# A strided local attention next to a long convolution on one core: four of the ten value-projection pairs move into the first weighting group

## The chip, the cores and the metric

One core of a Trainium2 chip runs the whole kernel. The metric is the device time in microseconds (us) of one execution; the figure that counts is the median over several executions. A hardware profile of one further execution is at hand: for every instruction its engine, start and duration, and what ended the idle time before it. Engines are named as the profile names them: PE multiplies matrices (PEld is its weight load), DVE works element by element, ACT copies out of PE's accumulator banks and computes exponentials, POOL and SP mostly issue DMA transfers.

## The reference

Two independent results stand side by side in the output. Part A is an attention with 32 heads of 20 channels over 2048 positions, in which each position looks at 8 positions, 0, 2, ... 14 back. Part B is a state-space convolution, which the kernel computes through a Fourier transform.

```python
# part A: x [1, 2048, 640], wqkv [640, 1920], wo [640, 640]
H = 32; Dh = 20; W, dil = 8, 2
q, k, v = split(x @ wqkv)                                # each [1, H, S, Dh]
idx = pos[:, None] - (arange(W) * dil)[None, :]          # mask = idx >= 0
logits = einsum("bhsd,bhswd->bhsw", q, k[idx]) * Dh**-0.5   # -1e9 where masked
attn = softmax(logits)
a = einsum("bhsw,bhswd->bhsd", attn, v[idx]).reshape(B, S, D) @ wo
# part B: y = irfft(rfft(u) * rfft(K)) + u * Dskip, with K from A, B, C, log_dt
out = concatenate([a, y], axis=-1)
```

## The kernel before

Until about 340 us of the span the kernel builds the convolution's tables and spectra and projects keys and queries. The change touches only what comes after. There, two kinds of work share the engines.

**Attention.** Positions are held in two halves of 256 columns for each of four stretches of 512 positions, and the offset w (0 to 7) picks the position that is looked at. `products(1, w)` on DVE multiplies queries of the second half by shifted keys, `logits(1, w)` on PE sums them over each head into scores, which ACT copies into `lsb` after every second w. `proj_v(d)` computes two of the 20 value channels, a *pair*, with 40 matmuls on PE into a two-bank accumulator tile, and ACT copies it to the tile `v2`. `v_halo` copies the 14 columns that a stretch needs from its neighbour, again by PE and ACT.

The softmax of a half is in two pieces. `softmax_a` takes the maximum over the 8 offsets and subtracts it (four DVE instructions), and ends with the exponential on ACT. `softmax_b` sums, takes the reciprocal and multiplies (five DVE instructions) and gives the weights `at`.

The *weighting* is six groups of eight `av_step`s, one per offset. A step is one DVE multiplication of values by weights into a ring of six buffers, then 16 small matmuls on PE that add the result into two two-bank tiles `ps_o`. After the eighth step ACT copies both tiles to `o`. The groups take the columns and channel blocks (0, 256, 0, 2), (0, 128, 2, 3), (128, 128, 2, 3), (256, 128, 0, 4), (256, 256, 4, 1), (384, 128, 0, 4): first column, columns, first block of four channels, blocks. Groups one to three use the weights of the first half, the others those of the second. `out_proj(q)` gives eight pieces, each five matmuls on PE, one copy and, every second piece, a store.

**Convolution.** `Inverse.parts()` is a list of 24 *parts*: each is 12 or 8 small matmuls on PE from a loaded tile `Z` and one copy to `ysb`; every third part stores. `load(qr)` brings in a quarter of the spectrum for six parts: 15 transfers of 128 KB, on the SP queue, or split over the SP and POOL queues for the first and the last quarter.

**What sets the order.** A planner orders the instructions of each engine when the program is built, mostly by their order in the source, but it may let an instruction pass others that it expects to wait. `keep_in_program_order` takes that freedom away for one instruction; `in_order()` switches it on for all matmuls that follow. At run time every engine, and each DMA queue, works through its list in order, and a wait holds what stands behind it.

**Accumulator banks.** Two-bank tiles (`big`, for `ps_v` and `ps_o`) come from three slots in turn, single banks (`one`, for the scores, `ps_ib`, `ps_op` and the halo) from two. A slot is free again when ACT has copied it. While a weighting group holds two of the three slots, one is left for value pairs.

**Other buffers.** `wo`, the output projection's weights, takes the place of `wv`, the value weights; the last quarter of `Z` takes the place of `xT`, the transposed input. Both places become free with the last value pair.

Of the kernel before, what the change touches and what calls it, by code (L numbers as in the profile page):

```python
# [10 lines left out]
A = mybir.AluOpType  # L11
ACT = mybir.ActivationFunctionType
AX = mybir.AxisListType
bf16 = mybir.dt.bfloat16
f32 = mybir.dt.float32

NCH = 5
# [385 lines left out]
class Attention:  # L403
# [146 lines left out]
    def softmax_b(self, hf):  # L550
        nc, lsb = self.nc, self.lsb[hf]
        TT = lambda o, a, b, op: nc.vector.tensor_tensor(out=o, in0=a, in1=b, op=op)
        tr = self.ta.tile([128, 4, 256], f32, name="tree", tag="TA0")
        TT(tr[:], lsb[:, 0:4], lsb[:, 4:8], A.add)
        TT(tr[:, 0:2], tr[:, 0:2], tr[:, 2:4], A.add)
        TT(tr[:, 0], tr[:, 0], tr[:, 1], A.add)
        nc.vector.reciprocal(out=tr[:, 1], in_=tr[:, 0])
        if hf == 0:
            self.AP_ = self.ta.tile([128, 4, 2048], bf16, name="atp", tag="R1")
        self.at[hf] = self.AP_[:, hf].rearrange("p (w i) -> p w i", w=W)  # L560
        TT(self.at[hf], lsb, tr[:, 1].unsqueeze(1).to_broadcast([128, W, 256]), A.mult)

    def open_out(self, a2):
        nc = self.nc
        self.o = a2.tile([128, 5, S], bf16, name="o")
        self.o4 = self.o[:].rearrange("p j (s i) -> p j s i", s=4)
        self.wo = self.ta.tile([128, 5, D], bf16, name="wo", tag="TX")
        wsrc = self.A_wo.rearrange("(h j dd) e -> dd h j e", j=5, dd=4)
        for dd in range(4):
            nc.gpsimd.dma_start(out=self.wo[32 * dd:32 * dd + 32], in_=wsrc[dd])  # L570
        self.ob = self.ta.tile([128, 6, D], bf16, name="ob", tag="cT")
        ring = self.ta.tile([128, 4, 2048], bf16, name="prod2", tag="R0")
        self.ring = [self.AP_[:, 2], self.AP_[:, 3]] + [ring[:, i] for i in range(4)]

    def av_step(self, i0, ni, j0, nj, w):

        nc = self.nc
        MM = self.MM
        at, n = self.at[i0 // 256], nj * ni
        if w == 0:  # L580
            self.ops = [self.big("ps_o") for _ in range(2)]
        p2 = self.ring[self.nav % 6][:, 0:4 * n]
        self.nav += 1
        off = HALO + i0 - DIL * w
        nc.vector.tensor_tensor(out=p2.rearrange("p (d i) -> p d i", i=ni), in0=self.v2[:, 4 * j0:4 * j0 + 4 * nj, off:off + ni],  # L585
                                in1=at[:, w, i0 % 256:i0 % 256 + ni].unsqueeze(1).to_broadcast([128, 4 * nj, ni]), op=A.mult)
        p2v = p2.rearrange("p (j dd i) -> p dd j i", dd=4, i=ni)
        for sc in range(4):
            for dd in range(4):
                sl = slice(32 * sc, 32 * sc + 32)  # L590
                MM(self.ops[sc // 2][32 * dd:32 * dd + 32, sc % 2, 0:n].rearrange("p (j i) -> p j i", i=ni), lhsT=self.ident[sl, sl], rhs=p2v[sl, dd],
                   start=(w == 0), stop=(w == W - 1), tile_position=(32 * sc, 32 * dd), skip_group_check=True)
        if w == W - 1:
            for f, p in enumerate(self.ops):
                nc.scalar.copy(out=self.o4[:, j0:j0 + nj, 2 * f:2 * f + 2, i0:i0 + ni], in_=p[:, :, 0:n].rearrange("p s (j i) -> p j s i", i=ni))  # L595
# [66 lines left out]
def body(tc, ctx, pools, prm, B_u, B_Dskip, Sd, Zd, UDd, A_x, A_wqkv, A_wo, out_a, out_b):  # L662
    nc = tc.nc
# [13 lines left out]
    with tc.tile_pool(name="prep_b", bufs=1) as pb, tc.tile_pool(name="prep_c", bufs=1) as pc, tc.tile_pool(name="prep_a", bufs=1) as pa, tc.tile_pool(name="psum_p", bufs=2, space=bass.MemoryType.PSUM) as psp:  # L677
        pools.update(prep_a=pa, prep_b=pb, prep_c=pc)
        B, fill = partB_prep(tc, dict(pools, psum=psp), prm)
# [17 lines left out]
    att = Attention(tc, pools, A_x, A_wqkv, A_wo, out_a, psk, psg)  # L697
# [86 lines left out]
    a2 = ctx.enter_context(tc.tile_pool(name="a2", bufs=1, side="right", reuse_waits="tile"))  # L784
# [3 lines left out]
    for w in range(W):  # L788
        if w >= 2:
            att.products(1, w)  # L790
        att.logits(1, w)
        if w == 2:
            att.softmax_b(0)
        att.proj_v(2 * w)
        if w == 3:
            att.proj_v(16)
        if w == 5:
            att.proj_v(18)
            att.v_halo(0, 8)
    att.v_halo(8, 8)  # L800
    att.v_halo(16, 4)
    att.in_order()
    inv.open_rows()
    inv.load(1)
    parts = inv.parts()
    rest = []

    def fill(some, n=1):
        for f in some[0:n]:
            f()  # L810
        del some[0:n]

    for w in range(W):
        if w < 2:
            fill(parts, 3 - w)
        elif w > 4:
            fill(parts)
        if w == 0:
            att.open_out(a2)
        att.av_step(0, 256, 0, 2, w)  # L820
        if w == 2:
            att.softmax_a(1)
        elif w == 4:
            att.softmax_b(1)
    LOADS = {(d, w + 2 * (qr == 3)): (qr, c) for c, (d, w) in enumerate(((0, 0), (0, 4), (1, 0), (1, 4), (None, 0))) for qr in (2, 3)}
    for i0, ni, j0, nj, done in ((0, 128, 2, 3, 0), (128, 128, 2, 3, 1), (256, 128, 0, 4, None), (256, 256, 4, 1, 2), (384, 128, 0, 4, 3)):
        for w in range(W):
            att.av_step(i0, ni, j0, nj, w)
            if (done, w) in LOADS:
                qr, c = LOADS[done, w]  # L830
                inv.load(qr, c, c + 1)
            if done == 2 or done == 0 and w % 2 == 1:
                fill(parts)
            elif done == 0:
                pass
            else:
                fill(rest)
                if done == 3 and w % 2 == 0:
                    fill(parts)
        if done is not None:  # L840
            rest += att.out_proj(done, done == 3)
    for f in parts + rest:
# [4 lines left out]
def kernel(  # L847
# [28 lines left out]
    Zd = dpool.tile([NCH, 128, 4096], bf16, name="Zdram")  # L876
    UDd = dpool.tile([NCH, 128, 2048], bf16, name="UDdram")
    body(tc, ctx, pools, prm, B_u, B_Dskip, Sd, Zd, UDd, A_x, A_wqkv, A_wo, out_a, out_b)


# [28 lines left out]
```

## Time and profile before

| what | us |
|---|---|
| median of 3 runs | 439.84 (439.48 to 441.04) |
| the profiled execution | 438.98 |
| its span, first to last instruction | 437.2 |
| busy: PE / DVE / ACT / POOL | 358.4 / 391.3 / 314.0 / 44.5 |
| mean granted PE clock | 0.916 of full speed |

The profile's page lists busy times, the span in 40 slices, the chain of waits that ended last and the costliest groups. A row of the timeline gives the start, the duration, the engine, the line, the operation with its result and operands, the number of instructions merged and, in brackets, the idle time of the engine before it and what ended that. A row of the windows view gives, for a stretch of time, the busy time of each engine with the number of its instructions, then the PE clock that was granted as a share of full speed, the busy share of the DMA engines and the GB/s that they moved.

### The profile page before, as it was taken

How to read it: one execution, taken by the hardware profiler on the slowest of the kernel's cores; microseconds unless marked ns; L12 is line 12 of the kernel's file. 1: busy time of each engine (PE TensorE's matmuls, PEld its weight loads, DVE VectorE, ACT ScalarE, POOL GpSimd, SP SyncE). 2: the span in 40 equal slices, each digit the busy share in tenths (PEclk: the TensorE clock that was granted, in tenths of full speed). 3: DMA queues.
4: the chain of work that ended last, by engine and by line, in shares of the span. 5: the costliest groups of instructions: out<-in, count | busy, mean ns of one | idle time of the engine just before them, and what ended most of it. 6: DMA issues, size and time to landing. Idle time of an engine off the chain costs nothing.

```text
span 437.2 us, 17687 instructions
## 1 busy us (share of the span) xinstructions
PE 358.4 (82%) x8041; PEld 241.1 (55%) x8041; DVE 391.3 (89%) x386; ACT 314.0 (72%) x570; POOL 44.5 (10%) x85
## 2 busy tenths in 40 slices
PE   1397659989886998879778799999899897399995
PEld 0145546866863677556665665545555674134443
DVE  7889999999997999999999989946978989999751
ACT  3974998889999899979997845342858344544663
POOL 7440000000000000000010000400001204102110
PEclk9996577999999898889999899999999999659999
DMA  5569102163233402324079933500210907957343
GB/s 143 186 141 200 18 3 109 39 227 94 99 123 123 97 28 98 144 103 99 27 258 241 236 75 135 178 0 3 67 32 1 265 17 201 228 141 225 96 107 114
DMA packets 45131, 51.62 MB, mean 118 GB/s; under 512 B 31376, under 2 KB 38992, under 8 KB 42368
## 3 DMA queue, kind: packets, MB, share of 16 engines
q1 hardware_dynamic: 41520, 41.41, 35.4%
q0 software_dynamic: 3392, 8.95, 7.0%
q8 instruction: 63, 1.03, 1.0%
q10 hardware_dynamic: 144, 0.12, 0.1%
q14 instruction: 12, 0.10, 0.1%
HBM read 28.03 MB, written 18.35 MB: 106 GB/s over the span
## 4 chain that ended last, share of the span: by engine, by line
PE 49%; ACT 29%; DVE 14%; issue 5%; DMA 1%; SPq 1%; DVEq 0%; ACTq 0%
ACT R L222 10%; ACT A L338 6%; PE ps_k L318 6%; PE ps_ph L247 6%; PE ps_k L323 6%; PE ps_op L420 6%; PE ps_k L470 4%; PE ps_q L488 4%; PE ps_ph L250 4%; ACT Sg L344 4%; PE ps_f L343 4%; PE ps_v L501 2%; DVE prod L521 2%; ACT Z L375 2%; PE ps_o L420 2%
## 5 line engine op out<-in xcount | busy, mean ns | idle before, releaser
L305 DVE TENSOR_TENSOR Y<-F,G 128x3072 bf16<-128x3072 bf16 x60 | 102.9, 1751 | 0.6 <-PE ps_k L323 0.6
L222 ACT ACTIVATE R<-LPC 128x192 bf16<-128x192 f32 x225 | 59.3, 358 | 0.1
L247 PE MATMUL ps_ph<-LPC 128*128 128x256 bf16 (+1 forms) x200 | 41.5, 311 | 17.3 <-DMA LPC<-lo 8.7
L318 PE MATMUL ps_k<-Y,X 128*32 128x64 bf16 x1920 | 47.2, 239 | 7.3 <-DVE Y L305 3.8
L323 PE MATMUL ps_k<-Y,X 64*32 64x64 bf16 x1920 | 43.8, 233 | 3.4 <-issue 3.3
L344 ACT CAST Sg<-ps_f 128x1024 bf16<-128x1024 f32 x40 | 37.6, 1027 | 7.3 <-PE ps_f L343 7.3
L318 PEld LDWEIGHTS <-X 128*32 128x32 bf16 x1920 | 32.1, 117 | 17.4 <-issue 9.0
L343 PE MATMUL ps_f<-A,T 128*128 128x128 bf16 x320 | 27.3, 259 | 14.9 <-ACT A L338 14.2
L338 ACT CAST A<-ps_f 128x1024 bf16<-128x1024 f32 x40 | 37.6, 1036 | 0.7 <-PE ps_f L337 0.6
L271 DVE TENSOR_TENSOR X<-R,TX 128x1536 bf16<-128x1536 bf16 x40 | 36.4, 951 | 0.0
L323 PEld LDWEIGHTS <-X 64*32 64x32 bf16 x1920 | 29.6, 113 | 12.1 <-issue 4.4
L255 ACT ACTIVATE TX<-ps_ph 128x864 bf16<-128x864 int16 (+1 forms) x40 | 31.9, 867 | 5.3 <-DVE X L271 2.5
L343 PEld LDWEIGHTS <-T 128*128 128x128 bf16 x320 | 25.6, 119 | 16.1 <-issue 14.9
L585 DVE TENSOR_TENSOR prod<-v,atp 128x2048 bf16<-128x2048 bf16 (+2 forms) x32 | 31.3, 1018 | 2.0 <-PE ps_o L420 1.8
L255 ACT ACTIVATE TA<-ps_ph 128x768 bf16<-128x768 int16 x40 | 30.6, 822 | 3.4 <-PE ps_ph L250 3.0
L250 PE MATMUL ps_ph<-LPC 128*64 128x128 bf16 (+1 forms) x400 | 29.6, 249 | 0.0
L247 PEld LDWEIGHTS <-LPC 128*128 128x128 bf16 x200 | 15.0, 102 | 25.9 <-issue 19.1
L420 PE MATMUL ps_op<-wo,o 128*128 128x320 bf16 x160 | 28.5, 315 | 0.8 <-ACT o L595 0.4
L358 DVE TENSOR_TENSOR P<-P,Sg 128x4096 bf16<-128x4096 bf16 x10 | 22.9, 2288 | 4.1 <-DMA P<-Sdram 3.2
L250 PEld LDWEIGHTS <-LPC 128*64 128x64 bf16 x400 | 15.2, 118 | 19.1 <-issue 18.9
L611 ACT CAST ob<-ps_op 128x320 bf16<-128x320 f32 x28 | 11.9, 431 | 19.0 <-PE ps_op L420 17.3
L337 PE MATMUL ps_f<-BD,U 128*64 128x128 bf16 x320 | 19.4, 285 | 6.1 <-ACT A L338 3.3
(129 smaller groups left out, 661.2 us busy)
## 6 DMA issues: line engine op xcount, KB each, us to landing
Sdram<-Sg SPq DMA_DIRECT2D x5, 1024.0 KB
P<-Sdram SPq DMA_DIRECT2D x5, 1024.0 KB
P<-Sdram SPq DMA_DIRECT2D x10, 512.0 KB
Zdram<-Z SPq DMA_DIRECT2D x5, 1024.0 KB
Z<-Zdram SPq DMA_DIRECT2D x30, 128.0 KB
U<-in_B_u_dram SPq DMA_DIRECT2D x4, 640.0 KB
UDdram<-UD SPq DMA_DIRECT2D x10, 256.0 KB
out_dram<-ysb SPq DMA_DIRECT2D x32, 80.0 KB
```

What stands on the lines that cost most here:

```text
L222: nc.scalar.activation(out=R[:, :, e, :], in_=src, func=ACT.Exp, scale=m)
L247: MM(o[:, :, 0:32], lhsT=L[:, 0:128], rhs=rhs, start=first, stop=last, skip_group_check=True)
L250: MM(o[64 * hh:64 * hh + 64, :, 32:48], lhsT=L[:, 128:192], rhs=rhs[:, :, 16 * hh:16 * hh + 16], start=False, stop=last, skip_group_check= ...
L255: last = nc.scalar.activation(out=dst[:, qs, e0:e0 + 2 * n, :].rearrange("p q (b e) f -> p b e q f", b=2), in_=words.rearrange("p b (e q f ...
L271: TT = lambda o, a, b, op: V.tensor_tensor(out=o, in0=a, in1=b, op=op)
L305: nc.vector.tensor_tensor(out=Y[:].rearrange("p q (b a) f -> p q b a f", a=8), in0=fa, in1=gb, op=A.mult)
L318: MM(ps[32 * g:32 * g + 32, t], lhsT=X[:, q, 2 - k, :, f], rhs=Ys[k][:, q, :, f], start=(t == 0 and k == 0), stop=False, tile_position=(0, ...
L323: MM(ps[32 * g:32 * g + 32, t], lhsT=X[hb, q, 2 - k, :, f], rhs=Ys[k][hb, q, :, f], start=False, stop=(k == 2), tile_position=(64 * (g // ...
L338: nc.scalar.copy(out=A1[:, :, 32 * b:32 * b + 32].rearrange("p k (j g) -> p k j g", g=4), in_=ps[:].rearrange("p j k g -> p k j g"))
L343: last = MM(ps[:, kk], lhsT=C["T2"][:, 8 * b + kk, :], rhs=A1[:, 8 * b + kk, :], start=(kk % 4 == 0), stop=True, skip_group_check=True)
L344: nc.scalar.copy(out=Sg[:, :, 8 * b:8 * b + 8, :], in_=ps[:].rearrange("p k (j g) -> p j k g", g=4))
L420: self.MM = lambda *a, **k: self.tc.keep_in_program_order(self.nc.tensor.matmul(*a, **k))
```

## The change

- The loop over the scores of the second half projects six value pairs (0, 2, ... 10) in place of ten, and copies only the first halo (8 channels). Pairs 12, 14, 16 and 18 stand in the first weighting group, ahead of its steps 0, 2, 3 and 5. One halo of 12 channels follows step 7, in place of two of 8 and 4 ahead of the weighting.
- All multiplications of the weighting are kept in program order, so none passes the score products.
- `softmax_a(1)` stays behind step 2 of the first group. `softmax_b(1)` moves from step 4 of the first group to step 3 of the third, and its first addition is kept in program order.
- Parts: six in the first group (before, eight), six in the second (four), four in the third (none), eight in the fifth (eight), none in the sixth (four).
- Output pieces: the first eight, spread one per step over the third group before, now come as three in its steps 0 to 2 and five at step 3.
- Loads of the last two quarters: one column block (three transfers) every second step from step 4 of the first group to step 6 of the third. The load of `wo` moves from the head of the weighting to behind the new halo.

```diff
     def softmax_b(self, hf):
-        TT(tr[:], lsb[:, 0:4], lsb[:, 4:8], A.add)
+        first = TT(tr[:], lsb[:, 0:4], lsb[:, 4:8], A.add)
+        if hf == 1:
+            self.tc.keep_in_program_order(first)
...
     def open_out(self, a2):
-        self.wo = self.ta.tile([128, 5, D], bf16, name="wo", tag="TX")
-        wsrc = self.A_wo.rearrange("(h j dd) e -> dd h j e", j=5, dd=4)
-        for dd in range(4):
-            nc.gpsimd.dma_start(out=self.wo[32 * dd:32 * dd + 32], in_=wsrc[dd])
...
+    def open_wo(self):
+        self.wo = self.ta.tile([128, 5, D], bf16, name="wo", tag="TX")
+        wsrc = self.A_wo.rearrange("(h j dd) e -> dd h j e", j=5, dd=4)
+        for dd in range(4):
+            self.nc.gpsimd.dma_start(out=self.wo[32 * dd:32 * dd + 32], in_=wsrc[dd])
...
     def av_step(self, i0, ni, j0, nj, w):
-        nc.vector.tensor_tensor(out=p2.rearrange("p (d i) -> p d i", i=ni), in0=self.v2[:, 4 * j0:4 * j0 + 4 * nj, off:off + ni],
+        ins = nc.vector.tensor_tensor(out=p2.rearrange("p (d i) -> p d i", i=ni), in0=self.v2[:, 4 * j0:4 * j0 + 4 * nj, off:off + ni],
                                 in1=at[:, w, i0 % 256:i0 % 256 + ni].unsqueeze(1).to_broadcast([128, 4 * nj, ni]), op=A.mult)
+        self.tc.keep_in_program_order(ins)
...
         att.logits(1, w)
         if w == 2:
             att.softmax_b(0)
-        att.proj_v(2 * w)
-        if w == 3:
-            att.proj_v(16)
-        if w == 5:
-            att.proj_v(18)
+        if w < 6:
+            att.proj_v(2 * w)
+        if w == 4:
             att.v_halo(0, 8)
-    att.v_halo(8, 8)
-    att.v_halo(16, 4)
...
-    for w in range(W):
-        if w < 2:
-            fill(parts, 3 - w)
-        elif w > 4:
-            fill(parts)
-        if w == 0:
-            att.open_out(a2)
-        att.av_step(0, 256, 0, 2, w)
-        if w == 2:
-            att.softmax_a(1)
-        elif w == 4:
-            att.softmax_b(1)
-    LOADS = {(d, w + 2 * (qr == 3)): (qr, c) for c, (d, w) in enumerate(((0, 0), (0, 4), (1, 0), (1, 4), (None, 0))) for qr in (2, 3)}
-    for i0, ni, j0, nj, done in ((0, 128, 2, 3, 0), (128, 128, 2, 3, 1), (256, 128, 0, 4, None), (256, 256, 4, 1, 2), (384, 128, 0, 4, 3)):
+    att.open_out(a2)
+    GROUPS = ((0, 256, 0, 2, None), (0, 128, 2, 3, 0), (128, 128, 2, 3, 1), (256, 128, 0, 4, None), (256, 256, 4, 1, 2), (384, 128, 0, 4, 3))
+    LOADS = {4 + 2 * n: (2 + n // NCH, n % NCH) for n in range(2 * NCH)}
+    for group, (i0, ni, j0, nj, done) in enumerate(GROUPS):
         for w in range(W):
+            if group == 0:
+                if w in (1, 3, 6):
+                    fill(parts, 2)
+                if w in (0, 2, 3, 5):
+                    att.proj_v(12 + 2 * (0, 2, 3, 5).index(w))
             att.av_step(i0, ni, j0, nj, w)
-            if (done, w) in LOADS:
-                qr, c = LOADS[done, w]
+            if 8 * group + w in LOADS:
+                qr, c = LOADS[8 * group + w]
                 inv.load(qr, c, c + 1)
-            if done == 2 or done == 0 and w % 2 == 1:
-                fill(parts)
-            elif done == 0:
-                pass
-            else:
-                fill(rest)
-                if done == 3 and w % 2 == 0:
-                    fill(parts)
+            if group == 0:
+                if w == 2:
+                    att.softmax_a(1)
+                elif w == 7:
+                    att.v_halo(8, 12)
+                    att.open_wo()
+            elif group == 1:
+                if w > 1:
+                    fill(parts)
+            elif group == 2:
+                if w < 3:
+                    fill(rest)
+                elif w == 3:
+                    att.softmax_b(1)
+                    fill(rest, 5)
+                else:
+                    fill(parts)
+            elif group == 4:
+                fill(parts)
+            else:
+                fill(rest)
```

More of the change, by code (lines that the diff above doesn't have):

```diff
@@ L566, in open_out @@
         self.o4 = self.o[:].rearrange("p j (s i) -> p j s i", s=4)
+        self.ob = self.ta.tile([128, 6, D], bf16, name="ob", tag="cT")
+        ring = self.ta.tile([128, 4, 2048], bf16, name="prod2", tag="R0")
+        self.ring = [self.AP_[:, 2], self.AP_[:, 3]] + [ring[:, i] for i in range(4)]
+    def open_wo(self):
         self.wo = self.ta.tile([128, 5, D], bf16, name="wo", tag="TX")
@@ L569, in open_out @@
         for dd in range(4):
-            nc.gpsimd.dma_start(out=self.wo[32 * dd:32 * dd + 32], in_=wsrc[dd])
-        self.ob = self.ta.tile([128, 6, D], bf16, name="ob", tag="cT")
-        ring = self.ta.tile([128, 4, 2048], bf16, name="prod2", tag="R0")
-        self.ring = [self.AP_[:, 2], self.AP_[:, 3]] + [ring[:, i] for i in range(4)]
+            self.nc.gpsimd.dma_start(out=self.wo[32 * dd:32 * dd + 32], in_=wsrc[dd])
     def av_step(self, i0, ni, j0, nj, w):
```

## The prediction

> **What bounds the kernel now.** Times are on the profiled execution's own clock: its span is 437.2 us, and the median of the runs shown, 439.84, stands 2.6 above that. The changed program's instruction lists equal the old ones until about 338 us, so I read the tail alone: first the timeline of DVE and ACT, then PE's, then the granted clock in windows, then the chain of waits.
>
> ```profile
> 353.81 5.55 DVE L521 TENSOR_TENSOR prod<-qT,kT 128x5120 bf16<-128x5120 bf16 x2
> 361.20 1.23 DVE L585 TENSOR_TENSOR atp<-v,atp 128x2048 bf16<-128x2048 bf16 x1 [1.83 <-ACT v L515]
> 362.34 3.49 DVE L585 TENSOR_TENSOR prod<-v,atp 128x2048 bf16<-128x2048 bf16 x3
> ...
> 369.20 2.29 DVE L542 TENSOR_TENSOR lsb<-lsb,tree 128x2048 f32<-128x2048 f32 x1
> ...
> 371.58 1.91 ACT L548 ACTIVATE lsb<-lsb 128x2048 f32<-128x2048 f32 x1 [2.19 <-DVE lsb L542]
> 373.40 1.49 ACT L653 CAST ysb<-ps_ib 128x480 bf16<-128x480 f32 x3
> ...
> 373.99 0.43 PE L420 MATMUL ps_ib<-Z,HB 96*32 96x160 bf16 x8 [3.08 <-ACT ysb L653]
> ...
> 385.75 3.56 DVE L585 TENSOR_TENSOR prod<-v,atp 128x1536 bf16<-128x1536 bf16 x4
> ...
> 405.50 0.69 DVE L585 TENSOR_TENSOR prod<-v,atp 128x1024 bf16<-128x1024 bf16 x1 [0.46 <-PE ps_o L420]
> ```
>
> DVE is full up to 405 us but for the halo (1.83) and the exponential (0.90). ACT's exponential (371.58) waits for DVE's subtraction, the copies of the parts wait behind it in ACT's list, and PE, whose next bank they free, stands still for 3.08. From 405 us it is DVE that waits for PE: the bound has changed hands. Why PE is late there, the clock says:
>
> ```profile
> 370.66:374.07 3.41, 0.34 (x25) 0.17 (x8) 2.51 (x3) 2.49 (x3) 1.12 (x3) 1.00 1.04 222
> 374.07:377.48 3.41, 0.94 (x24) 0.19 (x23) 3.41 (x5) 0.76 (x2) 0.53 (x1) 0.50 1.09 246
> ...
> 391.14:394.55 3.41, 3.41 (x42) 1.29 (x26) 3.41 (x5) 0.77 (x2) 0.57 (x1) 0.50 0.57 132
> 394.55:397.96 3.41, 3.41 (x65) 1.63 (x63) 3.41 (x4) 1.27 (x3) 0.56 (x1) 1.00 0.82 250
> ```
>
> After a window with PE busy 0.34 of 3.41 the grant falls to half and stays there for six windows. The grant changes on a grid of 3.41 us (118.07, 374.07 and 394.55 lie on it). In the third group an output piece and a step take 1.51 + 0.54 on PE, later 0.85 + 0.38. PE comes to the fourth group at 400.2, though DVE made its first product by 395.6; from there PE sets the pace, 25.7 us to the end of the last step's matmuls:
>
> ```profile
> 424.50 0.80 PE ps_op L420 x5
> ...
> 426.12 0.93 ACT o L595
> 427.04 0.05 issue
> 427.09 0.86 PE ps_op L420 x5
> ```
>
> The last `ps_o` ends at 425.9; copies, nine pieces and stores after it take 437.2 - 425.9 = 11.3, which the change leaves as it is.
>
> **The change, along the path.** *Scores.* The weighting's first product (1.14 from start to start) no longer passes the score products, which so end at 358.2, not 359.4. Four pairs (2.17 us each in the chain of waits) leave PE's list ahead of the scores, which were late by them: the last scores reach `lsb` at 358.2 + 0.7 + 0.6 = 359.5, in place of 364.5, before DVE asks for them. Three steps (3.49) bring DVE to 361.7, `softmax_a` (1.22 + 0.69 + 0.42 + 2.29, and 0.1 between) to 366.4.
>
> *The pairs and the exponential.* In the built program, ACT's list in the first group is:
>
> ```
> lsb1 copy | ps_v pair 12 | part 0 | part 1 | EXP | ps_v pair 14 | part 2 | part 3 | ps_v pair 16 | ps_v pair 18 | part 4 | part 5 | o | o | halo
> ```
>
> Pair 14's copy stands behind the exponential, and with `ps_o` in two of three slots pair 16 waits for that copy. PE is through pair 12 at 361.1, with parts 0 and 1 (0.7, and 0.5 for the loads' semaphores, as at 367.5 now) and two steps, pair 14 at 365.1, step 2 and parts 2 and 3 at 366.0. Then it waits: exponential 366.5 to 368.4, copy 1.01 (as all ten L503), so pair 16 runs 369.4 to 371.6, its copy ends at 372.7, pair 18 runs to 374.9. ACT: copy, two parts (1.07 + 0.56 + 0.42) to 377.0, two `o` copies (1.93) to 378.9, halo (0.26 for 112 columns, 0.36 for 168) to 379.3. DVE was through the group's eight steps at 366.4 + 5 x 1.16 = 372.2; the second group's step 0 needs pair 18 and waits until 376.0, its step 1 reads the halo and starts at 379.3. That is 3.8 + 2.4 = 6.2 us of new DVE stall.
>
> *DVE from there.* 7 + 4 steps at 0.89 (3.56 for four), `softmax_b` unmixed 1.23 + 0.68 + 0.42 + 1.75 + 2.28 = 6.4 with a gap, four steps 3.6: group four starts at 379.3 + 9.8 + 6.4 + 3.6 = 399.1. Its PE work starts a step later, 400.3: the time at which PE starts it now. The gain comes after it: 9.24 (group four), 5.9 (five: 1.52 and 1.43 for two), 9.24, then 0.43 of matmuls: last `ps_o` at 424.0, against 425.9. PE keeps that pace, 0.36 + 0.79 = 1.15 a step against DVE's 1.155, since group six loses its four parts and five is covered by DVE. End: 424.0 + 11.3 = 435.3.
>
> *The clock.* PE's idle 366.0 to 369.4 is as long as a window. Unseen here is where the windows lie and what grant follows. Lower bound nothing: a window with 1.71 of 3.41 busy (220.47) kept its grant. Upper bound: all at half speed, 2 x 2.17 for the pairs, and the three steps and two parts behind them (3 x 0.36 + 0.7, so 3.6 at half speed where ACT's 2.05 sets now) 1.6 more: 5.9. A window with 1.78 busy (114.66) did lose it, and so did the 3.08 above, so I take one window at half speed: 1.7. A second fall is likely around 380, when PE has little to do; then the third group's pieces start at 1.45. Their 7.6 us (4 x 0.31 + 8 x 0.79) with 5.1 us at half speed (5.5 now, 389.1 to 394.55) become 10.2 and end where `softmax_b` does (6.4 + 3.6): hidden, but without that cover 2.5.
>
> *Loads, halo, order.* `wo`: four transfers on POOL behind pair 18, issued by 376.6 + 2.3 = 378.9, landed in at most 7.3 (4.6 to 7.3 now): 386.2, wanted at 388. Queued behind it, the last quarter's POOL transfers are wanted after 410. SP: a store that waits for part 5's copy (378.6) stands ahead of 12 loads of 0.6, the last landed after at most 8.2, 394.0; PE wants them from 398. Both at nothing; a load late by x costs at most x. The two halos become one, 0.2 of PE. Parts moved to groups two and three lie beside DVE steps of 0.89, at 0.31 + 0.32 warm and 1.0 at half speed.
>
> Sum: 437.2 - 1.9 (435.3) + 1.7 = 437.0; plus 2.6 for the median: **439.6**, no change that can be told (within 0.5%, 2.2 us).
>
> The Trainium skill (TensorE: Matmul & The Clock Gate, "Why this matters for your kernels" and Part 1) has the clock fall after one idle window of about 3.4 us. By that rule a gap of 3.4 hardly ever holds a whole idle window, and the sum is 435.3 (437.9). The trace disagrees: 10% and 52% busy windows lost the grant.
>
> **Rivals.** (A) *Half speed throughout, slower.* If the grant does not return with pair 16, both pairs pay: 435.3 + 4.3 = 439.6, median 442.2; with the pieces behind them 441.2, median 443.8. For: now the grant took six windows to return, though PE was busy 3.02 and 3.38 in two. Against: pairs are dense, and such work (118.07, half speed, 3.41 busy) brought it back at once. It decides from two windows at half speed on. (B) *The grant holds*: 435.3, median 437.9. For: the window at 220.47. (C) *The pairs do not wait*, because the exponential is done when pair 14 is: then only the `o` copies and the halo hold DVE, 372.6 + 1.9 + 0.4 = 375.0 in place of 379.3, the end is 435.3 - 4.3 = 431.0 and the median 433.6. Against: it needs `softmax_a` 3.3 us earlier, and DVE's list has no gap to give. (D) *A load is late*: `wo` or the third quarter by 3 us, median 442.6. For: DMA engines were over 1.0 busy at 374; against: margins of 2 and 4 us.
>
> **How the numbers follow.** Forecast 0.40, A 0.26, B 0.20, C 0.07, D 0.07. Beside its own range (438.2 to 441) it takes in B and most of A: 436.8 to 443.4, leaving out C and the ends of A and D. Faster by over 0.5% (under 437.6): C and half of B, 0.17. Slower (over 442.0): A and D less the part within, 0.31. The rest, 0.52, is the same.
>
> **What would show it.** PE waiting some 3 us or more for ACT's copy of a value pair just after the exponential; DVE idle about 4 and 2 us ahead of steps 0 and 1 of the second group; no DVE wait for `ps_o` in the fifth group; last `ps_o` near 425.6; half clock near 370 and again near 382. It is wrong if pair 14's copy runs ahead of the exponential, if DVE is held elsewhere by over 1 us, or if PE still sets the end by more than a step.

## The result: slower by 0.6%

| | median, us | executions |
|---|---|---|
| before, measured again beside it | 441.81 (438.24 to 446.03) | 22 |
| after | 444.13 (439.88 to 449.4) | 22 |
| ratio after to before | 1.0059 (95%: 1.003 to 1.0088) | |

The forecast was 439.6 against a median of 439.84, no change. Of the 4.5 us between 444.13 and 439.6, 2.0 are the kernel before, whose median is 2.0 higher in this series; the ratio says that the change itself costs 2.6 us. The ratios, here and below, leave out executions over 1.5% above the fastest of their kernel. After's profiled execution took 441.29 us, its span is 439.5.

DVE's timeline of after (start, duration, engine, line, operation with result and operands, count, and in brackets the idle time ahead of it and what ended that):

```profile
357.94 2.35 DVE L589 TENSOR_TENSOR atp<-v,atp 128x2048 bf16<-128x2048 bf16 x2
...
363.78 2.29 DVE L542 TENSOR_TENSOR lsb<-lsb,tree 128x2048 f32<-128x2048 f32 x1
...
376.01 0.96 DVE L589 TENSOR_TENSOR prod<-v,atp 128x1536 bf16<-128x1536 bf16 x1 [4.26 <-ACT v L503]
378.84 2.69 DVE L589 TENSOR_TENSOR prod<-v,atp 128x1536 bf16<-128x1536 bf16 x3 [1.87 <-ACT v L515]
...
398.31 2.35 DVE L589 TENSOR_TENSOR atp<-v,atp 128x2048 bf16<-128x2048 bf16 x2
...
411.93 1.32 DVE L589 TENSOR_TENSOR prod<-v,atp 128x1024 bf16<-128x1024 bf16 x2 [0.65 <-PE ps_o L420]
413.50 2.36 DVE L589 TENSOR_TENSOR prod<-v,atp 128x2048 bf16<-128x2048 bf16 x2 [0.25 <-PE ps_o L420]
```

The scores' products end at 358.0, the softmax's subtraction at 366.1. The two new stalls stand where they were forecast, 4.26 + 1.87 = 6.1 us (forecast 6.2), and the fourth group starts at 398.3 (forecast 399.1 without its clock term). ACT's timeline shows why:

```profile
366.17 1.91 ACT L548 ACTIVATE lsb<-lsb 128x2048 f32<-128x2048 f32 x1 [3.01 <-DVE lsb L542]
367.99 0.99 ACT L503 CAST v<-ps_v 128x1024 bf16<-128x1024 f32 x1
...
374.97 1.01 ACT L503 CAST v<-ps_v 128x1024 bf16<-128x1024 f32 x1 [2.49 <-PE ps_v L420]
...
376.65 1.96 ACT L600 CAST o<-ps_o 128x1024 bf16<-128x1024 f32 x2
378.45 0.35 ACT L515 CAST v<-ps_h 128x168 bf16<-128x168 f32 x1
```

The copy of pair 14 (367.99) stands behind the exponential, pair 18's copy ends at 376.0 and the halo's, behind two `o` copies, at 378.8: at both moments DVE goes on. Up to here the forecast holds. PE's timeline shows what it did not have:

```profile
369.03 2.39 PE L420 MATMUL ps_v<-xT,wv 128*32 128x512 bf16 x40 [3.27 <-ACT v L503]
...
386.42 1.08 PE L420 MATMUL ps_o<-prod,ident 32*32 32x384 bf16 x11
389.09 0.51 PE L420 MATMUL ps_o<-prod,ident 32*32 32x384 bf16 x5 [1.59 <-issue]
389.53 1.51 PE L420 MATMUL ps_op<-wo,o 128*128 128x320 bf16 x5
...
401.81 0.41 PE L420 MATMUL ps_o<-atp,ident 32*32 32x512 bf16 x8 [0.31 <-ACT o L600]
...
417.84 1.09 PE L420 MATMUL ps_o<-prod,ident 32*32 32x512 bf16 x16
418.87 1.51 PE L420 MATMUL ps_op<-wo,o 128*128 128x320 bf16 x5
420.32 0.65 PE L420 MATMUL ps_o<-prod,ident 32*32 32x512 bf16 x16
420.90 1.27 PE L420 MATMUL ps_op<-wo,o 128*128 128x320 bf16 x5
```

At 387.5 PE stops after 11 of a step's 16 matmuls and waits 1.59 us for nothing that the profile can name ("issue"): no semaphore holds the next matmul of the same step. In group four PE does the first half of a step at 401.09, waits 0.31 for ACT's copy of `o` and goes on at 401.81, although DVE's first product was there at 398.31 + 1.2 = 399.5: 2.3 late. In group six the first two steps with their pieces take 4.26 us (417.84 to 422.10) and not 2.3. The last `ps_o` ends at 428.3, against 425.9 before. What slows group six is the clock. Here are windows of 3.41 us with the busy time of each engine (PE, its weight load, DVE, ACT, POOL), the granted PE clock, the DMA engines' busy share and GB/s that they moved:

```profile
367.18:370.59 3.41, 1.56 (x29) 1.50 (x32) 3.41 (x5) 2.59 (x4) 0.00 (x0) 1.00 0.57 163
...
377.42:380.83 3.41, 0.85 (x40) 0.36 (x39) 1.99 (x3) 1.39 (x3) 3.39 (x7) 1.00 1.05 260
380.83:384.24 3.41, 3.41 (x104) 1.34 (x101) 3.41 (x5) 1.54 (x3) 0.00 (x0) 0.50 1.09 279
...
391.07:394.48 3.41, 3.41 (x42) 1.35 (x40) 3.38 (x2) 0.85 (x2) 0.77 (x2) 0.50 0.65 164
...
411.55:414.96 3.41, 2.65 (x120) 1.50 (x123) 2.78 (x4) 2.78 (x6) 0.54 (x1) 1.00 0.23 71
414.96:418.38 3.42, 3.42 (x115) 1.40 (x104) 3.42 (x4) 2.54 (x6) 0.00 (x0) 0.50 0.59 128
```

In this execution the grant survives the pairs' wait (1.56 busy at 367.18) and falls after 377.42, as forecast, and again after 411.55, in group five, which was not forecast. No load made PE late: the landings in the trace show the last transfer of the third quarter (issued at 389.10) there by 393.3, and PE comes to it at 398.9. (The 398.9 that two expectations below take for this landing is that of a later transfer on the same semaphore.)

### The profile page after: what moved, and what is told of

It reads as the page before. It is cut to its first block, busy times and chain, and to the rows that moved or that the text cites. A ratio compares the mean times of both kernels' runs of the same rounds, so it can differ in the third digit from the quotient of the medians.

```text
span 439.5 us, 17685 instructions
## 1 busy us (share of the span) xinstructions
PE 361.0 (82%) x8037; PEld 242.6 (55%) x8037; DVE 391.4 (89%) x386; ACT 313.8 (71%) x569; POOL 45.1 (10%) x85
## 4 chain that ended last, share of the span: by engine, by line
PE 48%; ACT 30%; DVE 11%; issue 7%; DMA 2%; SPq 1%; DVEq 0%; ACTq 0%
ACT R L222 10%; ACT A L338 6%; PE ps_k L318 6%; PE ps_k L323 6%; PE ps_ph L247 6%; PE ps_op L420 5%; PE ps_k L470 4%; PE ps_q L488 4%; PE ps_ph L250 4%; PE ps_f L343 4%; ACT Sg L344 4%; DVE prod L521 3%; PE ps_o L420 3%; ACT Z L375 2%; DVE X L271 2%
## 5 line engine op out<-in xcount | busy, mean ns | idle before, releaser
L247 PEld LDWEIGHTS <-LPC 128*128 128x128 bf16 x200 | 14.9, 102 | 24.9 <-issue 9.6
```

The lines of the kernel that those rows point to most:

```text
L247: MM(o[:, :, 0:32], lhsT=L[:, 0:128], rhs=rhs, start=first, stop=last, skip_group_check=True)
```

## The experiments

Executions already differ by up to 7.4 us before the first edited instruction, so profiles are compared from a point that all share: the start of the reciprocal in the first half's `softmax_b`. Times behind it, each from one profiled execution; the ratios come from many:

| kernel | ratio to before (95%) | reciprocal at | group four on DVE | last `ps_o` | end of span |
|---|---|---|---|---|---|
| before | 1 | 336.7 | 57.7 | 89.2 | 100.5 |
| after | 1.0059 (1.003 to 1.0088) | 336.5 | 61.8 | 91.8 | 103.0 |
| after, again | 1.0039 (0.9986 to 1.0093) | 340.1 | 63.3 | 93.0 | 104.2 |
| exponential behind the pair | 0.9951 (0.9914 to 0.9988) | 336.9 | 59.1 | 86.1 | 97.3 |
| exponential and halo | 0.9922 (0.9885 to 0.996) | 336.8 | 57.1 | 86.1 | 97.3 |
| added matmuls | 1.0092 (1.0052 to 1.0132) | 342.8 | 63.5 | 99.3 | 110.5 |
| pairs back | 0.9874 (0.9791 to 0.9957) | 339.1 | 58.5 | 87.1 | 98.4 |
| pairs alone | 1.0059 (1.0013 to 1.0105) | 337.7 | 61.3 | 92.5 | 103.8 |
| loads later | 0.997 (0.9921 to 1.002) | 336.1 | 63.0 | 90.8 | 102.1 |
| groups mixed | 0.9877 (0.982 to 0.9934) | 340.2 | 57.1 | 84.1 | 95.3 |
| transfers added | 1.0045 (1.0011 to 1.0079) | 340.0 | 63.5 | 94.0 | 105.2 |
| later and mixed | 1.0013 (0.9972 to 1.0053) | 335.4 | 63.5 | 89.8 | 101.1 |
| all of it | 0.9911 (0.9872 to 0.995) | 337.8 | 57.1 | 86.5 | 97.8 |
| pairs back, later, mixed | 0.9912 (0.9877 to 0.9948) | 340.6 | 58.5 | 84.8 | 96.1 |

**The same kernel again.** No edit.

> The changed kernel once more, unedited, as the base for its companions. Its profiled execution lost 2.3 us to the old one's at the end of the last step's matmuls though DVE reached group four at 398.3, 0.8 ahead of the forecast. Theory C (clock): where the grant falls differs from execution to execution, so the half-speed stretches (380.8 to 394.5 and 415.0 to 421.8 in the first profile) move or are missing here, and the last ps_o moves with them by 1 to 3 us from 428.3. Theory W (waits): the two DVE stalls (4.3 and 1.9 us) and PE's wait of 3.3 for pair 16 are here again within 0.3 us, and the last ps_o ends at 428.3 within 0.5. Time: 1.003 to 1.009 of the kernel before by either.

The waits are here again (PE 3.27, DVE's second stall 1.88), and so is the gap marked issue, 1.40. But the clock fell in the pairs' wait this time. PE's timeline of this execution:

```profile
372.62 3.92 PE L420 MATMUL ps_v<-xT,wv 128*32 128x512 bf16 x40 [3.27 <-ACT v L503]
```

Its windows, with the columns as above:

```profile
369.01:372.42 3.41, 0.34 (x20) 0.23 (x9) 3.41 (x4) 2.67 (x2) 0.00 (x0) 1.00 0.63 202
372.42:375.84 3.42, 3.22 (x32) 1.80 (x35) 2.92 (x3) 0.93 (x3) 0.00 (x0) 0.50 0.69 176
```

Pair 16 takes 3.92, DVE's first stall is 5.80 in place of 4.26, 1.5 more. It fell there in six of the seven profiles that have this wait (the first profile of after is the seventh). Both theories have a part: the waits repeat, and the end behind the reciprocal moves with the clock, by 1.2 us.

**The waits taken away.** `softmax_a(1)`'s exponential is pinned behind what stands ahead of it in the source:

```diff
-        nc.scalar.activation(out=lsb, in_=lsb, func=ACT.Exp)
+        late = nc.scalar.activation(out=lsb, in_=lsb, func=ACT.Exp)
+        if hf == 1:
+            self.tc.keep_in_program_order(late)
```

> The changed kernel with the second half's exponential pinned behind pair 14's copy in ACT's list; nothing else differs. Both theories: PE's wait of 3.3 us ahead of pair 16 and DVE's of 4.3 ahead of group two's first step are gone, DVE's stall ahead of its second step (halo behind the o copies) stays, about 3. Theory W (these waits set the end): the time falls by 2 to 3 us against the changed kernel. Theory C (PE at half speed in groups three and six sets the end, whatever DVE does): by under 1 us.

and in the second kernel the halo goes ahead of parts 4 and 5 as well:

```diff
+                if w == 6:
+                    att.v_halo(8, 12)
                 if w in (1, 3, 6):
                     fill(parts, 2)
...
                 elif w == 7:
-                    att.v_halo(8, 12)
                     att.open_wo()
```

> The same, and the last halo's matmuls issued before parts 4 and 5 and steps 6 and 7, so that its copy stands ahead of the o copies. Both theories: no DVE stall over 0.5 us is left ahead of group two, DVE reaches group four about 6 us earlier than 398.3. Theory W: the time falls by 4 to 6 us against the changed kernel (to 434 to 436 on the span's clock) and the kernel is faster than the one before by about 1%. Theory C: by under 2 us. A load late (third quarter, last landed at 398.9 in the first profile): PE waits for Z at part 12 by the difference and the gain stops at about 3.

PE's timeline of the first:

```profile
366.44 2.39 PE L420 MATMUL ps_v<-xT,wv 128*32 128x512 bf16 x40 [0.29 <-ACT v L503]
```

ACT's timeline of the second:

```profile
365.24 1.01 ACT L503 CAST v<-ps_v 128x1024 bf16<-128x1024 f32 x1 [1.82 <-PE ps_v L420]
366.42 1.94 ACT L548 ACTIVATE lsb<-lsb 128x2048 f32<-128x2048 f32 x1 [0.17 <-DVE lsb L542]
...
373.89 0.30 ACT L515 CAST v<-ps_h 128x168 bf16<-128x168 f32 x1 [0.35 <-PE ps_h L420]
```

DVE's timeline of the second:

```profile
373.58 3.56 DVE L591 TENSOR_TENSOR prod<-v,atp 128x1536 bf16<-128x1536 bf16 x4 [1.57 <-ACT v L503]
```

The copy costs the exponential 0.17, PE's wait shrinks from 3.27 to 0.29, and the halo no longer stalls DVE; 1.6 of the first stall is left, where none was expected. By the ratios of this series the edits take 0.9% and 1.2%, 4 and 5 us, off the changed kernel (1.0039): theory W, the first by more than its 2 to 3. In their profiles the second gains nothing on the first (97.3 both), since DVE's 2.0 us lead at group four is lost to a fall of the clock in group five that the first execution did not have.

**Matmuls added for the clock.** 21 matmuls whose result nobody reads:

```diff
+            if group == 1 and w < 2:
+                warm((7, 6)[w])
+            if group == 4:
+                warm(1)
             att.av_step(i0, ni, j0, nj, w)
```

> The changed kernel with 21 matmuls added whose result nobody reads: 7 ahead of group two's first step, 6 ahead of its second, one ahead of each step of group five (512 columns, all 128 rows and columns; 0.21 us each at full speed). They fill the window of 377.42 (busy 0.25) and the fifth group (window 411.55, busy 0.78). Theory C: the grant stays full from there on, group three's pieces take 0.8 and not 1.5, group six's first steps 1.15, and the time falls by 1.5 to 3 us, less 1 to 1.5 for the added matmuls in group five. Theory W: no gain, 0 to 2 us slower by the added work.

By the ratio this is 1.5 to 2.3 us slower than the two series of after, near theory W's 0 to 2, but the profiled execution shows more than the added work. (It took 455.08, the longest of the twelve, whose median is 444.95, so its sizes are not the usual ones.) The grant stayed through group two (windows 385.85 and 389.26 at 1.00), and then PE, its timeline says, stood still in the longest gap marked issue of all profiles:

```profile
397.81 0.32 PE L420 MATMUL ps_ib<-Z,HB 96*32 96x160 bf16 x3 [4.18 <-issue]
```

That cost the clock again, from 396.1, and in groups five and six it was half from 423.4 to 437.1. The nameless gap came although PE ran at full clock ahead of it: half speed is not its cause.

**The pairs alone, and all but the pairs.** The first kernel is after with its value pairs and halos where they were; the second is before with the pairs, the halo and the load of `wo` as in after. The start of the first one's edit:

```diff
-        if w < 6:
-            att.proj_v(2 * w)
-        if w == 4:
-            att.v_halo(0, 8)
+        att.proj_v(2 * w)
+        if w == 3:
+            att.proj_v(16)
+        if w == 5:
+            att.proj_v(18)
+            att.v_halo(0, 8)
+    att.v_halo(8, 8)
+    att.v_halo(16, 4)
```

> The changed kernel with its four value pairs and the last two halos back ahead of the weighting, as in the kernel before; the parts, the loads, softmax_b in pieces and the pinned steps stay. Theory W (the pairs' waits are what the change costs): the stalls of 4.3 and 1.9 us ahead of group two are gone; group one starts later, as in the kernel before, and the time is 0.99 to 1.00 of the kernel before. Theory R (the rest of the change costs it: loads placed earlier and crowded, PE slowed in groups two, three and five): 1.003 to 1.01, as the changed kernel.

> The kernel before with the four pairs moved into group one and the halo and the loads of wo behind them, and nothing else of the change. Pair 14's copy stands behind the exponential here too. Theory W: PE waits about 3 us for pair 16, DVE some 4 to 6 us ahead of group two, and the time is 1.005 to 1.012 of the kernel before. Theory R: within 0.3% of the kernel before.

The pairs' move alone costs 0.6% (0.1 to 1.1), all the rest gains 1.3% (0.4 to 2.1, six executions): theory W on both, though the first interval ends too near theory R's 0.3% to exclude it without the waits in the profile. In the kernel with the pairs alone PE waits 4.55 for pair 16 and DVE 3.06 + 2.01 ahead of group two.

**Loads later.** The last quarter's loads at steps 18 to 22, POOL's part pinned, so behind the first output stores:

```diff
-    LOADS = {4 + 2 * n: (2 + n // NCH, n % NCH) for n in range(2 * NCH)}
+    LOADS = {(4 + 2 * n if n < NCH else 13 + n): (2 + n // NCH, n % NCH) for n in range(2 * NCH)}
...
+                if qr == 3 and (c + ri) % 2:
+                    self.att.tc.keep_in_program_order(ins)
```

> The changed kernel with the last quarter's loads at steps 18 to 22 in place of 14 to 22 by twos, those on POOL's queue pinned behind its first stores, so that six transfers fewer run between 377 and 391. Theory F (PE's gap of 1.4 to 1.9 us marked issue in group two's last step is a fetch of its instructions queued behind these transfers): the gap is gone or under 0.5, the third quarter lands 1 to 2 us earlier than 398.9, PE starts group four by 400.5 in place of 401.8, and the time falls by 1 to 1.5 us. Theory G (the gap comes of something else): it stays, and the time is the changed kernel's within 0.5 us, or later if part 18 then waits for its loads.

and, the other way round, six transfers of 256 KB added to POOL's queue:

```diff
                 inv.load(qr, c, c + 1)
+                if qr == 3 and c < 3:
+                    for k in range(2):
+                        tc.keep_in_program_order(nc.gpsimd.dma_start(out=spare[2 * c + k], in_=Zd[c, :, 1024 * k:1024 * k + 1024]))
```

> The changed kernel with six transfers of 256 KB from DRAM to DRAM added on POOL's queue among the last quarter's loads (four of them between wo and the first output store); nobody reads what they write. Theory F (PE's gap marked issue in group two is its instruction fetch queued behind transfers): the gap grows from 1.4 to 1.9 us to 3 or more, and the time by 1.5 to 4 us. Theory G (the gap has nothing to do with transfers): it stays at 1.4 to 1.9 us and the time within 1 us, unless a load of the third quarter is late by more, which shows as PE's wait for Z.

With the loads later the step runs through, and PE waits for DVE at the head of group four. PE's timeline:

```profile
387.25 1.10 PE L420 MATMUL ps_o<-prod,ident 32*32 32x384 bf16 x16
388.28 1.51 PE L420 MATMUL ps_op<-wo,o 128*128 128x320 bf16 x5
...
400.39 0.72 PE L420 MATMUL ps_o<-atp,ident 32*32 32x512 bf16 x16 [0.34 <-DVE atp L589]
```

Against the other profile of after with a half-speed pair, 2.1 us are gone (104.2 to 102.1); by the ratios it is 3 to 4 us (0.997 against 1.0039 and 1.0059), more than the 1 to 1.5 expected, and that excess is not explained. With transfers added the gap did not grow: 0.99. That part of theory F fails. Its profile has a second gap marked issue, though, in group four, while POOL's transfers ran on from 399.4 to 413.2:

```profile
410.26 0.40 PE L420 MATMUL ps_o<-prod,ident 32*32 32x512 bf16 x6 [0.85 <-issue]
```

What PE waits for shows in the packets of the queue named instruction (the page's q8: 63 packets of 16 KB, on average one for 128 of PE's 8037 matmuls with their weight loads). In the fourteen profiles PE has 138 gaps over 0.2 us that are marked issue, 5 to 12 in each, and in every one it goes on 1.2 to 1.7 us after the end of an instruction packet (for 137 of them on q8, for one on the smaller queue q14, which has the same kind). So these gaps are PE waiting for its own instructions. The kernel before has ten of them, 7.1 us in all; the timeline of its PE, far ahead of the change, has

```profile
132.50 0.29 PE L318 MATMUL ps_k<-Y,X 128*32 128x64 bf16 x6 [1.17 <-issue]
```

with no data transfer under way in the 3 us ahead of the fetch: PE can run dry without any.

What made the fetch late in the tail is a matter of comparison. In the last four kernels of this table one fetch begins between the same two matmuls, right ahead of the 888th from the end, and that is taken for the place where it is due in all eleven. Nine have equally many matmuls, and two have four more, earlier:

```
kernel                     888th matmul   POOL's transfers   fetch starts    late   PE's gap
after                         383.2        376.5 to 386.8       386.4         3.2      1.59
after, again                  388.2        381.6 to 392.3       391.2         3.0      1.40
exponential behind the pair   380.9        374.2 to 385.5       384.2         3.3      1.92
transfers added               388.3        381.7 to 394.1       391.1         2.8      0.99
groups mixed                  382.7        377.5 to 387.1       384.8         2.1      0.40
exponential and halo          379.3        374.1 to 383.1       380.8         1.4       -
all of it                     379.4        375.2 to 380.4       380.1         0.7       -
loads later                   384.0        377.3 to 381.4       383.9          0        -
later and mixed               383.6        377.0 to 381.5       383.5          0        -
pairs back                    383.2        369.7 to 381.2       382.9          0        -
pairs back, later, mixed      384.1        371.1 to 378.1       383.7          0        -
```

Where POOL's transfers are over, the fetch starts at that matmul; where they still run, it starts 0.7 to 3.3 us late, and PE runs dry when that is over 2: in these five the gap is the lateness less 1.4 to 1.8. (With the added matmuls, which shift the count, it was 4.6 late and the gap 4.18. With the pairs alone, where the order of the parts differs, it began 1.5 behind the 888th, POOL's transfers running from 383.6 to 394.1, and PE did not run dry.) SP's transfers alone did not do it here: with the pairs back they kept all 16 DMA engines busy from 381 to 383, and the fetch of 382.9 was on time. So the gap is a late instruction fetch, and it goes with the load of `wo` and the last quarter's transfers that the last pair released together: with these fewer or earlier it is gone. How the queues are served, so why six more transfers did not delay it further, stays open.

**Groups mixed.** Three of group four's pieces exchanged for three of group five's parts, on top of the exponential and the halo; then the same with after as it is and the loads later; then everything together; then, without the exponential and the halo, the loads later and the exchange with the pairs back:

```diff
-            elif group == 4:
-                fill(parts)
-            else:
-                fill(rest)
+            elif group < 5:
+                fill(rest if (group == 3) != (w in ((2, 4, 7), (1, 3, 5))[group - 3]) else parts)
+            else:
+                fill(rest)
```

> The kernel with the exponential behind pair 14's copy and the halo ahead of the o copies, and besides three of group four's output pieces exchanged for three of group five's parts. PE's work in group five rises from some 5 to 6.2 us beside 5.9 of DVE's. Theory C (the grant falls in group five since parts and steps there are small tiles, and group six's first steps then take 1.5 and not 1.15): no half speed from 410 to 417 in any profile, and 0.5 to 1.5 us less than the kernel without the exchange (436.5, ratio 0.9922). If the fall costs nothing, the same or up to 0.5 us more.

> The changed kernel with its pairs and the exponential as they are, the last quarter's loads later and three pieces and parts of groups four and five exchanged: what the forecast left out (fetch gap, fall in group five) taken away, what it counted (the pairs' wait, half speed beside it, two DVE stalls) left in. If the forecast's own terms were right, the last ps_o ends 87.3 to 89 us after the reciprocal of softmax_b's first half (forecast 424.0 to 425.7 less 336.7; the changed kernel 91.8 and 93.0), and the time is 0.995 to 1.00 of the kernel before. If they were not, it stays at 90 to 93.

> Exponential behind pair 14's copy, halo ahead of the o copies, loads later, groups mixed. If the fetch gap (0.4 us still in the mixed kernel) and the crowded loads cost anything there, 0.5 to 1.5 us less than the mixed kernel: 0.983 to 0.987 of the kernel before, last ps_o 83 to 84 after the reciprocal. If they are covered: the same as the mixed kernel, 0.9877, 84.1.

> The pairs back ahead of the weighting, loads later, groups mixed: the same two remedies without the pairs' move. Theory W says that the move of the pairs is worth something once nothing waits for them (scores end 1.2 us earlier, DVE's stalls of 1.5 and 1.0 in group one go): this one is 1 to 2 us slower than the kernel with all of it. If the move is worth nothing: the same within 0.5 us.

Windows of the kernel without the exchange (exponential and halo), in group five:

```profile
406.85:410.26 3.41, 2.71 (x136) 1.49 (x120) 3.26 (x4) 2.79 (x7) 0.54 (x1) 1.00 0.39 106
410.26:413.67 3.41, 3.41 (x75) 1.35 (x72) 3.41 (x4) 2.43 (x5) 0.00 (x0) 0.50 0.56 122
```

Windows of the mixed kernel, in group five:

```profile
406.35:409.76 3.41, 2.71 (x93) 1.39 (x78) 3.41 (x7) 2.64 (x5) 0.54 (x1) 1.00 0.63 153
409.76:413.17 3.41, 3.12 (x94) 1.65 (x93) 3.41 (x5) 2.08 (x6) 0.54 (x1) 1.00 0.10 19
```

Equally busy, 2.71, but with pieces among the parts the grant stays, and the last `ps_o` comes 2.0 us sooner at the same start of group four (57.1): the price of the second fall. It is the size expected or a little over. The stretch from DVE's start of group four to the last `ps_o` is 27.8 to 29.0 in three profiles in which the clock falls in group five (exponential and halo, pairs back, loads later), and 26.3 to 27.0 in the four in which it does not (exponential behind the pair, groups mixed, and the two mixed kernels below other than all of it). The ratios don't show it: the exchange moves them from 0.9922 to 0.9877 here, from 0.997 to 1.0013 with the loads later, and from 0.9874 to 0.9912 with the pairs back (the loads later as well), all within the intervals. So the price is that of a fall where it comes; that the exchange makes the kernel faster was not shown.

With the loads later and the groups mixed, after's pairs, exponential and halo unchanged, the ratio is 1.0013 (0.9972 to 1.0053): the forecast's "no change". Its last `ps_o` at 89.8 is 0.8 beyond the forecast's 89.0.

All of it together is no better than the mixed kernel, within the intervals. PE, no longer late, runs out of work while DVE computes `softmax_b`; its timeline:

```profile
392.46 0.39 PE L420 MATMUL ps_o<-prod,ident 32*32 32x384 bf16 x16 [2.36 <-DVE prod L591]
```

and the clock falls there, so that groups three and four run at half speed from 395.3 to 402.1. It falls once more, for the window from 408.9, in group five with its pieces among the parts: the exchange does not always keep the grant (it did in the other three mixed kernels, and without it the grant fell in group five in six of seven profiles). With the pairs back in place of the exponential and the halo the ratio is the same within 0.1%, so theory W's last claim, 1 to 2 us, is not borne out; intervals of 0.4% to each side don't exclude it. The best two, the mixed kernel and the one with the pairs back, 1.2 and 1.3% faster than before with six executions each, can't be told apart.

## Why the prediction was wrong

- *Pairs, exponential, halo, DVE's stalls*: right in mechanism and size (PE's wait 3.27 for 3.4, DVE 6.1 for 6.2, group four 0.8 sooner than 399.1). Taking the waits away made the kernel faster than before.
- *The clock term, 1.7, one window in the pairs' wait*: right as a frequent case (six of seven profiles; 1.2 to 1.7 us more of DVE's stall in the five of them with after's layout), absent from after's first profile. Rivals A (pairs at half speed throughout) and B (grant holds) bracket it; A never occurred. That A's 442.2 is next to the 442.4 that the ratio gives on the forecast's base (439.84 + 2.6) is chance.
- *The fall near 380, "hidden by `softmax_b`"*: it came, at 380.8, and was hidden as said, but only where the instruction fetch is on time (loads later: the fall at 379.9, and PE waits for DVE at group four).
- *"Both at nothing; a load late by x costs at most x"*: **this step failed first.** The loads were not late (the third quarter landed by 393.3, forecast 394.0). While they ran, bunched on POOL's queue behind the last pair, a fetch of PE's own instructions started 3.2 us late, PE stopped for 1.59, and came 2.3 us late to group four. Ten such gaps, 0.2 to 1.3 us each, stood in the profile of the kernel before, marked issue. Rival D had a load late by 3 us: the place nearly, not the mechanism.
- *"PE keeps that pace, ... five is covered by DVE"*: **this failed too.** DVE does cover group five at full speed, but in its small tiles the grant was lost (in six of the seven profiles with this group five), and group six's first two steps took 4.26 in place of 2.3, 2.0 more.

The sum after the fact, in after's first profile: from DVE's start of group four to the last `ps_o` 30.0 us (398.3 to 428.3), forecast 24.9 (399.1 to 424.0). Of the 5.1 more, 2.3 is PE's lateness at group four (0.31 of it the wait for ACT), 2.0 the second fall, and 0.8 group five at PE's own pace (417.84 - 411.17 = 6.7, forecast 5.9), with waits of 0.36 and 0.38 for ACT. Less 0.8 (DVE sooner) and 1.7 (no fall in the wait), that is the 2.6 between 428.3 and the forecast's 425.7.

## What to carry to other kernels

When work is moved that releases a buffer, look at everything that its release starts: a burst of transfers can be in time for its own readers and still hold up something that no tile names, here the instruction fetch, which shows as an engine's idle time marked issue in the middle of a row of equal matmuls. When a stall is costed, cost the clock in each later stretch where PE has only small tiles, not in the stall alone. And where a copy that frees an accumulator bank and a long activation share ACT, let the copy go first: it cost the exponential 0.17 us and saved PE 3.

## What the hardware did that was not expected

- PE fetches its instructions by DMA while the kernel runs, and its gaps marked issue are waits for them: all 138 of them end 1.2 to 1.7 us after an instruction packet. In the tail a fetch started up to 4.6 us after the matmul at which it seems due, while POOL's transfers ran.
- Busy time does not say what the clock will do. After 380.83 (3.41 of 3.41 busy with steps and parts) the grant stayed at half; after 391.07 (3.41 busy, mostly 128*128 pieces) it came back. It fell after 2.71 busy without pieces and stayed after 2.71 with some, but with all of it together it fell after 2.43 with part of a piece (405.51 to 408.92). The Trainium skill (TensorE: Matmul & The Clock Gate, Part 1, "What's actually happening") gives full speed after one busy window of about 3.4 us; the trace disagrees for windows filled with 32*32 and 96*32 tiles. Which measure decides was not settled: in the kernel before, 2.91 busy with such tiles (411.62) kept the grant.
